# Pooled attention and a SoLU layer on one core: a new order for the first 260 steps

## The chip, the cores and the metric

One NeuronCore of a Trainium2 chip runs the whole program. The metric is its time on the device in microseconds, the median of three runs. The engines are TensorE (PE in the rows), VectorE (DVE), ScalarE (ACT), GpSimd (POOL) and SyncE (SP); each runs its own instructions in order, and they meet at semaphores. All transfers of this kernel are issued from SP's queue, DMA transpositions among them.

## What is computed

```python
# q, k, v: 8 batches x 8 heads x 576 x 64, f32;  w_in 512x1024, w_out 1024x512
k_p = k.reshape(B, H, 72, 8, D).mean(axis=3)
v_p = v.reshape(B, H, 72, 8, D).mean(axis=3)
scores = scale * np.matmul(q, k_p.transpose(0, 1, 3, 2))
attn = np.exp(scores - np.max(scores, axis=-1, keepdims=True))
attn = attn / (np.sum(attn, axis=-1, keepdims=True) + 1e-09)
x = np.matmul(attn, v_p)            # to 4608 tokens x 512
h = x @ w_in
e = np.exp(h - np.max(h, axis=-1, keepdims=True))
solu = h * (e / (np.sum(e, axis=-1, keepdims=True) + 1e-09))
ln = (solu - mean) / np.sqrt(var + 1e-06) * g_ln
out = ln @ w_out
```

## The kernel before

The 4608 tokens are 36 tiles of 128. A group of nine tiles belongs to two batches: four tiles of the first, one that is half of each, four of the second. Every product is made with float16 pairs, a high and a low part, in three passes (high by high, high by low, low by high). The weights come from memory as 8-byte floats, in four quarters of 1 MB each, and are made into such pairs on the chip: ScalarE takes the exponent word (`w_exp`, line 522) and later a sum of magnitudes (`w_abs`), VectorE shifts and joins the words (`w_shift`, `w_tail`), the four bounds give one scale (`w_rmax`, `w_par` on TensorE, `w_all`, `wi_scale` or `wo_scale`), then ScalarE makes the high part (`w_hi`) and the low part comes over TensorE and ScalarE for w_in (`w_res`, `w_lo`) and from VectorE for w_out. `g_ln`, the layer's gain, is loaded by `load_g` (line 609) and enters w_out's scale.

A tile goes through these steps: `q_hi` (ScalarE) and `q_lo` (VectorE for the first four tiles, else POOL) make q's pair, `q_T` transposes it by DMA (line 751); `scores` on TensorE; `s_max`, `s_sub`, `s_exp`, `e_sum`, `e_rec`, `e_mul` make the softmax on VectorE and ScalarE; `e_hi` (ScalarE) and `e_lo` (POOL) its pair, `e_T` transposes it (line 843); `av` multiplies with v (line 853); `x_hi` (ScalarE) and `x_lo` (VectorE) make x's pair; `mm1` multiplies with w_in (line 885, three parts of eight matmuls); `h_max`, `h_exp`, `z_mul`, `z_hi`, `z_cen`, `z_lo`, `z_var` make the layer's z, `z_T` transposes it (line 960); `mm2` multiplies with w_out (line 1017); `o_evac` and `o_store` write the result. Per batch, POOL adds up the groups of eight of k and v (`pool_kv`, line 341, three levels for each of three pieces), VectorE and TensorE find a scale (`a_max`, `a_par`, `a_all`, `a_scale`), and `v_put` on POOL lays v out for `av` in `vb`. For tile 0, `mm1`'s third part needs all low parts of w_in and its second the low part of x.

Buffers set waits as well. The tag `h` in PSUM has two buffers, given in the order of use: four `w_res` of w_in, then `mm1` of tile after tile. The tags `x` (`av`, and the small products for scales) and `s` (`scores`) have one each. q's pairs have two, so `q_hi` waits for the transposition that read the buffer before.

The order of all work is written out by hand. Lines 1044 to 1400 list 2272 steps, each with its engine and what it depends on; `ORDER` (line 25) names them by number, and the loop at the end issues them in that order, so it is the order of each engine's instructions:

```python
    with tc.manual_schedule():
        for n in order:
            ops[n][3](*ops[n][4])
```

So TensorE, VectorE, ScalarE, POOL and SP each see the subsequence of `ORDER` that is theirs. In the kernel before, SP begins with three pieces of k, g, two halves of q (part 0, part 1), a small piece of v, four quarters of w_in, the first quarter of w_out, one half of v, q_T(0), the other half of v, the fourth quarter of w_out, q_T(1), the second quarter, q's mixed tile, the third quarter, a small piece of the next k, q_T(2), a small piece of the next v, e_T(0).

Of the kernel before, what the change touches and what calls it, by code (L numbers as in the profile page):

```python
# [25 lines left out]
    2, 0, 1, 12, 3, 4, 11, 50, 5, 6, 56, 57, 7, 53, 8, 58, 54, 13, 182, 51, 52, 9, 183, 55, 75, 65,  # L26
    59, 184, 113, 185, 76, 186, 60, 66, 187, 188, 61, 190, 77, 62, 63, 17, 64, 189, 191, 236, 192,
    18, 67, 237, 21, 10, 20, 16, 19, 238, 22, 68, 25, 24, 23, 26, 28, 29, 27, 30, 32, 31, 14, 94,
    33, 34, 69, 35, 36, 114, 282, 193, 283, 37, 47, 194, 72, 195, 48, 196, 95, 73, 44, 197, 131,
    74, 198, 41, 199, 70, 200, 15, 97, 71, 331, 134, 38, 284, 239, 115, 78, 201, 79, 39, 137, 240,  # L30
    203, 49, 204, 80, 241, 202, 205, 81, 242, 332, 206, 98, 82, 42, 243, 83, 244, 85, 381, 88, 245,
    89, 129, 99, 86, 90, 40, 382, 130, 246, 91, 333, 383, 102, 285, 384, 385, 93, 45, 386, 286,
    248, 87, 43, 103, 92, 96, 287, 101, 144, 207, 288, 247, 289, 208, 250, 46, 290, 210, 291, 209,
    249, 292, 251, 84, 106, 145, 252, 481, 163, 211, 293, 132, 294, 482, 146, 387, 133, 389, 334,
    107, 483, 104, 212, 390, 335, 484, 108, 336, 297, 296, 253, 213, 337, 164, 295, 254, 298, 338,
    138, 100, 256, 214, 339, 216, 340, 217, 135, 255, 215, 139, 136, 110, 218, 341, 111, 257, 141,
    391, 219, 342, 112, 220, 343, 344, 345, 299, 485, 223, 116, 346, 258, 300, 224, 105, 347, 302,
    117, 259, 227, 225, 303, 123, 226, 301, 486, 260, 109, 142, 229, 120, 304, 262, 221, 263, 487,
    126, 124, 140, 264, 348, 118, 143, 261, 265, 231, 119, 165, 147, 228, 157, 266, 232, 349, 128,
    158, 269, 350, 489, 122, 271, 148, 351, 125, 270, 127, 330, 121, 352, 274, 273, 305, 488, 272,  # L40
    149, 233, 306, 222, 308, 307, 150, 309, 151, 152, 230, 275, 310, 311, 267, 153, 353, 312, 160,
    154, 234, 268, 155, 315, 235, 277, 354, 316, 161, 156, 490, 313, 355, 278, 159, 357, 358, 356,
    388, 162, 359, 317, 319, 166, 537, 362, 279, 360, 276, 361, 491, 318, 314, 167, 392, 280, 492,
    321, 364, 393, 323, 168, 394, 538, 365, 493, 169, 170, 171, 324, 363, 395, 368, 366, 320, 396,
    539, 397, 325, 173, 398, 322, 399, 174, 176, 400, 367, 494, 326, 403, 370, 495, 401, 372, 402,
    496, 404, 178, 405, 175, 497, 373, 179, 636, 498, 377, 586, 499, 180, 327, 500, 177, 501, 374,
    281, 181, 504, 502, 587, 172, 406, 505, 588, 540, 407, 503, 541, 409, 369, 506, 443, 507, 542,
    444, 408, 543, 410, 436, 544, 328, 545, 546, 411, 547, 727, 548, 412, 551, 550, 508, 549, 413,
    552, 589, 509, 371, 553, 414, 590, 415, 511, 637, 416, 591, 380, 375, 417, 418, 592, 512, 419,
    510, 329, 437, 420, 638, 445, 554, 438, 593, 423, 376, 513, 378, 439, 594, 421, 595, 555, 728,  # L50
    425, 424, 596, 557, 427, 556, 597, 514, 599, 598, 428, 426, 729, 558, 515, 730, 516, 440, 429,
    731, 732, 517, 733, 639, 518, 422, 734, 600, 559, 640, 735, 601, 641, 441, 602, 431, 642, 456,
    560, 737, 379, 830, 519, 442, 561, 522, 563, 432, 738, 520, 562, 521, 430, 739, 564, 524, 603,
    565, 566, 523, 567, 831, 433, 604, 526, 525, 457, 643, 832, 644, 568, 606, 570, 645, 528, 646,
    605, 572, 571, 527, 446, 607, 434, 573, 649, 435, 784, 447, 608, 574, 647, 448, 449, 648, 569,
    450, 451, 651, 736, 452, 576, 650, 453, 578, 609, 575, 454, 652, 610, 529, 612, 579, 613, 614,
    459, 455, 615, 611, 577, 580, 530, 879, 617, 616, 462, 653, 581, 583, 460, 633, 532, 654, 463,
    655, 461, 464, 740, 458, 619, 785, 533, 741, 620, 465, 531, 786, 742, 466, 534, 467, 623, 743,
    632, 468, 469, 470, 744, 472, 622, 624, 621, 656, 745, 746, 747, 473, 584, 475, 474, 748, 787,
    749, 476, 751, 535, 657, 788, 750, 752, 789, 702, 753, 618, 658, 790, 929, 479, 791, 625, 792,  # L60
    478, 627, 793, 794, 682, 477, 659, 795, 585, 480, 833, 582, 798, 660, 628, 662, 661, 663, 664,
    834, 880, 796, 835, 754, 686, 881, 665, 836, 666, 629, 797, 626, 755, 635, 756, 669, 683, 837,
    757, 671, 670, 838, 667, 684, 630, 930, 758, 799, 931, 689, 800, 674, 932, 933, 934, 703, 839,
    840, 687, 759, 634, 1029, 842, 471, 631, 690, 841, 688, 783, 672, 882, 760, 677, 673, 883, 845,
    675, 668, 884, 844, 801, 761, 885, 763, 678, 705, 764, 802, 886, 935, 887, 691, 762, 765, 685,
# [108 lines left out]
def kernel(  # L174
# [102 lines left out]
    bat = {b: {} for b in range(B)}  # L277
# [1165 lines left out]
```

## Time and profile before

| | |
|---|---|
| time, median of 3 runs | 480.87 us (480.17 to 481.0) |
| the profiled execution, its time | 481.14 us |
| its span, first to last instruction | 479.4 us |
| TensorE busy | 443.1 us, 92% of the span |
| VectorE, ScalarE, POOL busy | 341.4, 354.1, 349.7 us |
| granted TensorE clock | 1.000 over the span |
| DMA share, share of the 16 engines' span | 80.2% |

The span is the part between the first and the last instruction of the profiled execution; 1.74 us lie around it. A busy share is a mean over the whole span, while the work differs: in the first 45 us TensorE is far from full, and from 120 us on it has hardly a gap. In the rows, a timeline's line gives the start, the time, the engine, the line of the kernel, the tiles written and read, and in brackets how long the engine stood before it and what ended that wait. `xN` is a group of N instructions in one line. Starts are from the span's start.

### The profile page before, as it was taken

The numbers are of one execution on the slowest core, as the hardware profiler recorded it, in microseconds if no ns is written. First come the engines' busy times: TensorE is split into PE (matmuls) and PEld (weight loads), VectorE is DVE, ScalarE is ACT, GpSimd is POOL, SyncE is SP. The second block draws the span as 40 slices with busy tenths as digits, with TensorE's granted clock in tenths as the row PEclk, the third lists the DMA queues.
The fourth block names the chain that finished last, engine by engine and source line by source line (L and its number), as shares of the span: only waits on it lengthen the run. The fifth ranks groups of instructions, "written<-read, shape, count | busy, mean of one in ns | idle before, by whom it ended". The sixth has DMA issues, their size and how long they took to land.

```text
span 479.4 us, 9043 instructions
## 1 busy us (share of the span) xinstructions
PE 443.1 (92%) x3100; PEld 230.1 (48%) x3100; DVE 341.4 (71%) x835; ACT 354.1 (74%) x593; POOL 349.7 (73%) x489
## 2 busy tenths in 40 slices
PE   0167999999999999999999999999999999999996
PEld 0033544555455555554545544555545554545462
DVE  2989998599668876677668975787657886783620
ACT  1789999769976687767876698677776688666751
POOL 6256789968999897997989568996999538535340
PEclk9999999999999999999999999999999999999999
DMA  8999864899989999889978888889997648435451
GB/s 253 418 348 214 227 120 109 174 236 230 194 210 204 218 167 235 173 209 198 208 164 198 187 196 177 200 178 220 195 203 166 151 101 145 111 85 130 92 137 58
DMA packets 201390, 89.14 MB, mean 186 GB/s; under 512 B 177664, under 2 KB 186112, under 8 KB 200832
## 3 DMA queue, kind: packets, MB, share of 16 engines
q1 hardware_dynamic: 201344, 88.57, 80.2%
q8 instruction: 24, 0.39, 0.4%
q14 instruction: 22, 0.18, 0.1%
HBM read 36.70 MB, written 9.44 MB: 96 GB/s over the span
## 4 chain that ended last, share of the span: by engine, by line
PE 78%; DMA 8%; DVE 5%; ACT 5%; issue 2%; SPq 1%; POOL 0%; ACTq 0%; POOLq 0%
PE op L1017 35%; PE hp L885 34%; PE xp L853 6%; DMA qT<-q 4%; PE sc L763 3%; DMA eT<-e 2%; DMA qr<-in_q_dram 2%; DVE wo L689 1%; DVE m L895 1%; DMA zT<-z 1%; DVE u_wo L536 0%; ACT osb L1025 0%; ACT junk L965 0%; ACT xT L861 0%; ACT q L734 0%
## 5 line engine op out<-in xcount | busy, mean ns | idle before, releaser
L1017 PE MATMUL op<-wo,zT 128*128 128x512 f16 (+1 forms) x888 | 197.3, 373 | 1.4 <-DMA zT<-z 0.8
L885 PE MATMUL hp<-wi,xT 128*128 128x512 f16 x864 | 195.8, 379 | 2.7 <-ACT xT L861 2.7
L885 PEld LDWEIGHTS <-xT 128*128 128x128 f16 x864 | 82.7, 98 | 97.8 <-ACT xT L861 3.3
L1017 PEld LDWEIGHTS <-zT 128*128 128x128 f16 x888 | 84.4, 98 | 92.0 <-DMA zT<-z 1.9
L952 POOL TENSOR_TENSOR z<-z,z 128x512 f16<-128x512 f32 x71 | 82.2, 1169 | 42.5 <-ACT z L939 42.2
L895 DVE TENSOR_REDUCE m<-hp 128x1 f32<-128x1024 f32 x36 | 44.0, 1223 | 28.2 <-PE hp L885 28.1
L341 POOL TENSOR_TENSOR vr<-vr 128x512 f32<-128x512 f32 (+3 forms) x48 | 48.1, 1006 | 14.6 <-DMA vr<-in_v_dram 14.0
L832 POOL TENSOR_TENSOR e<-e,e 128x512 f16<-128x512 f32 x36 | 41.6, 1155 | 22.6 <-ACT e L825 22.4
L944 ACT ACTIVATE z<-z,sz 128x1024 f16<-128x1024 f32 x36 | 41.2, 1145 | 17.6 <-DVE z L930 17.4
L906 ACT ACTIVATE z<-hp,nb,Hb 128x1024 f32<-128x1024 f32 x32 | 38.4, 1199 | 15.0 <-DVE nb L898 14.2
L930 DVE SCALAR_TENSOR_TENSOR z<-hp,rs,z 128x1024 f32<-128x1024 f32 x36 | 46.1, 1280 | 3.4 <-ACT z L906 2.0
L341 POOL TENSOR_TENSOR kr<-kr 128x512 f32<-128x512 f32 (+3 forms) x48 | 42.3, 890 | 4.3 <-DMA kr<-in_k_dram 3.7
L774 DVE TENSOR_REDUCE mx<-sc 128x8 f32<-128x576 f32 x36 | 27.2, 754 | 23.8 <-PE sc L763 23.4
L939 ACT ACTIVATE z<-z,sz 128x1024 f32<-128x1024 f32 x36 | 41.1, 1143 | 0.7
L1025 ACT ACTIVATE osb<-op,f 128x512 f32<-128x512 f32 (+1 forms) x37 | 24.7, 667 | 20.0 <-PE op L1017 11.8
L853 PEld LDWEIGHTS <-vb 128*128 128x128 f16 x640 | 35.2, 98 | 8.8 <-DMA eT<-e 1.2
L853 PE MATMUL xp<-eT,vb 128*128 128x128 f16 (+1 forms) x640 | 38.2, 214 | 0.2
L965 ACT ACTIVATE junk<-z 128x1024 f16<-128x1024 f32 x36 | 37.7, 1047 | 0.2
L744 POOL TENSOR_TENSOR q<-qr,q 128x512 f16<-128x512 f32 x28 | 32.3, 1156 | 6.8 <-ACT q L734 6.8
L788 DVE TENSOR_REDUCE sc<-sc 128x8 f32<-128x576 f32 x36 | 27.4, 762 | 13.5 <-ACT sc L784 13.3
L861 ACT ACTIVATE xT<-xp 128x512 f16<-128x512 f32 x36 | 21.3, 592 | 15.3 <-PE xp L853 14.9
L763 PEld LDWEIGHTS <-qT 128*128 128x128 f16 (+1 forms) x640 | 23.1, 103 | 12.1 <-issue 3.8
(232 smaller groups left out, 588.2 us busy)
## 6 DMA issues: line engine op xcount, KB each, us to landing
kr<-in_k_dram SPq DMA_DIRECT2D x16, 512.0 KB, 4.4
qr<-in_q_dram SPq DMA_DIRECT2D x16, 512.0 KB, 4.9
vr<-in_v_dram SPq DMA_DIRECT2D x16, 512.0 KB, 4.9
out_dram<-osb SPq DMA_DIRECT2D x31, 256.0 KB, 3.0
wor<-in_moe_w_out_dram SPq DMA_DIRECT2D x4, 1024.0 KB, 9.2
wo<-in_moe_w_in_dram SPq DMA_DIRECT2D x2, 1024.0 KB, 8.2
wir<-in_moe_w_in_dram SPq DMA_DIRECT2D x2, 1024.0 KB, 12.1
out_dram<-osb SPq DMA_DIRECT2D x10, 128.0 KB, 2.3
```

The lines of the kernel that those rows point to most:

```text
L341: nc.gpsimd.tensor_tensor(out=dst, in0=src[:, :, :n], in1=src[:, :, n : 2 * n], op=ALU.add)
L832: nc.gpsimd.tensor_tensor(out=m[:, 1], in0=e_pair(i)[:, :, :P], in1=m[:, 0], op=ALU.subtract)
L853: nc.tensor.matmul(xp[:, c, lo:hi], lhsT=vb[b % 2][:, x, c].rearrange("p j d -> p (j d)"), rhs=eT[:, e, lo:hi], start=(n == 0), stop=(n == 3),
L885: nc.tensor.matmul(hp[:, f], lhsT=xT[:, xt, c], rhs=wi[:, wt, c, f * 512 : (f + 1) * 512], start=(part == 0 and n == 0), stop=(part == 2 a ...
L895: nc.vector.tensor_reduce(out=small(i, "m"), in_=tl[i]["hp"], axis=AX.XY, op=ALU.max)
L906: nc.scalar.activation(z, t["hp"], AF.Exp, bias=t["nb"], scale=hsc(i, 0), accum_out=small(i, "se"))
L930: nc.vector.scalar_tensor_tensor(out=t["z"], in0=t["hp"], scalar=t["rs"], in1=t["z"], op0=ALU.mult, op1=ALU.mult, accum_out=small(i, "sz"),)
L939: nc.scalar.activation(t["zf"], t["zf"], AF.Identity, bias=t["sz"], scale=-float(DFF))
L944: nc.scalar.activation(t["z16"][:, 0], t["zf"], AF.Identity, bias=t["sz"], scale=-float(DFF))
L952: eng.tensor_tensor(out=t["z16"][:, 1, fs], in0=t["zf"][:, fs], in1=t["z16"][:, 0, fs], op=ALU.subtract)
L965: nc.scalar.activation(junk, t["zf"], AF.Square, scale=DFF**-0.5, accum_out=small(i, "V"))
L1017: nc.tensor.matmul(op_, lhsT=zT[:, zt, c], rhs=wo[:, wt, c, cols(hf)], start=(part == 0 and n == 0), stop=(part == 2 and n == len(todo) - 1),)
```

## The change

The first 260 entries of `ORDER` are a new permutation of the same 260 steps; entry 261 and all behind it are as before. No step, duration or buffer is added or taken away. Two conditions in the code let a part that is not part 0 come first. By engine, what moves:

- SP: three pieces of k, q's part 1, q's part 0, the small piece of v, four quarters of w_in, q_T(0), both halves of v, q_T(1), the fourth and the first quarter of w_out, q's mixed tile, the second quarter, q_T(2), e_T(0), the third quarter, a small piece of the next k, g, q_T(3), e_T(1), and then the other loads of the next batch between e_T(2), q_T(4), z_T(0) and e_T(3).
- VectorE: q's two maxima and its scale before k's; `w_tail` of w_in's fourth quarter behind `s_sub`(1); tile 0's softmax around w_in's scale; `a_max` and `a_scale` of v ahead of tile 1's `s_max`; `w_tail` of w_out's third and fourth quarter ahead of `h_max`(0), where they stood behind `wo_scale`; the maxima of the next batch's q behind `z_mul`(0); g's maximum behind `h_max`(0) and its reduction (`g_all`) just ahead of `z_mul`(0).
- ScalarE: `s_exp`(0) ahead of w_in's high parts, `kv_ps` and `v_hi` of v sooner, `x_hi`(0) ahead of the low parts of w_in's fourth and third quarter, `w_exp` of w_out's third and fourth quarter between these two; `s_exp`(3) behind `x_hi`(1); `z_hi`(0), `z_cen`(0), `x_hi`(2) in this order, where it was `z_hi`(0), `x_hi`(2), `z_cen`(0).
- TensorE: w_in's `w_res` in the order of quarters 1, 2, 4, 3 (it was 4, 1, 2, 3), with `scores`(2) ahead of the last two and `av`(0) between them; `mm1`(0) is cut by `scores`(3) after its first part; g's product and w_out's `w_par` stand between the parts of `mm1`(1); then `mm1`(1)'s third part, `av`(2), `mm1`(2) (it was `av`(2), `mm1`(1)'s third part, `mm1`(2)).
- POOL: the additions in a slightly different order, `e_lo` and the additions for the next batch exchanged in places.

```diff
 ORDER = (
-    2, 0, 1, 12, 3, 4, 11, 50, 5, 6, 56, 57, 7, 53, 8, 58, 54, 13, 182, 51, 52, 9, 183, 55, 75, 65,
-    59, 184, 113, 185, 76, 186, 60, 66, 187, 188, 61, 190, 77, 62, 63, 17, 64, 189, 191, 236, 192,
-    18, 67, 237, 21, 10, 20, 16, 19, 238, 22, 68, 25, 24, 23, 26, 28, 29, 27, 30, 32, 31, 14, 94,
-    33, 34, 69, 35, 36, 114, 282, 193, 283, 37, 47, 194, 72, 195, 48, 196, 95, 73, 44, 197, 131,
...
+    2, 0, 50, 51, 56, 52, 1, 4, 183, 53, 57, 54, 3, 182, 58, 11, 184, 5, 55, 75, 65, 66, 76,
+    185, 186, 187, 188, 59, 60, 190, 191, 61, 62, 6, 7, 63, 64, 236, 8, 17, 192, 18, 20, 237,
+    189, 67, 19, 68, 193, 9, 77, 10, 21, 22, 25, 26, 24, 23, 28, 29, 27, 69, 30, 331, 31, 238,
+    194, 70, 72, 195, 196, 33, 71, 34, 35, 73, 74, 36, 282, 41, 197, 16, 198, 199, 200, 37, 239,
+    38, 201, 202, 78, 203, 44, 13, 131, 79, 283, 14, 80, 81, 240, 82, 83, 85, 94, 241, 242, 39,
+    42, 32, 284, 332, 205, 204, 243, 244, 245, 206, 381, 86, 84, 87, 89, 47, 88, 246, 15, 40,
+    95, 98, 382, 43, 383, 285, 286, 384, 48, 287, 247, 288, 97, 91, 90, 93, 92, 207, 96, 208,
+    134, 385, 289, 248, 386, 290, 12, 249, 49, 291, 99, 209, 250, 292, 101, 102, 45, 333, 210,
...
     def load_q(eng, b, part):
-        if part == 0:
+        if "q" not in bat[b]:
             bat[b]["q"] = p2.tile([P, H, 4, D], F32, tag="qr", name=f"qr{b}")
...
     def z_T(i, x):
         t = tl[i]
-        if x == 0:
+        if "zT" not in t:
             t["zT"] = p3.tile([P, 2, CO, P], F16, tag="zT", name=f"zT{i}")
```

In these numbers 5 to 8 are w_in's quarters, 13 to 16 w_out's, 9 to 11 v's pieces, 12 is g; 192, 238, 284 and 333 are q_T of tiles 0 to 3, 206 and 252 e_T of tiles 0 and 1.

## Rows read from the trace of the kernel before

**Rows 1.** Stretches: us, busy PE, PEld, DVE, ACT, POOL (instructions); clock, DMA share, GB/s.

```profile
6.00:8.00 2.00, 0.00 (x0) 0.00 (x0) 0.00 (x0) 0.00 (x0) 1.92 (x4) 1.00 0.91 197
16.00:18.00 2.00, 0.00 (x0) 0.00 (x0) 1.86 (x3) 2.00 (x4) 0.00 (x0) 1.00 0.99 418
30.00:40.00 10.00, 6.71 (x34) 2.75 (x32) 9.84 (x23) 9.93 (x16) 4.81 (x8) 1.00 1.16 312
120.00:240.00 120.00, 120.00 (x850) 62.33 (x849) 87.68 (x219) 91.82 (x155) 108.58 (x149) 1.00 0.95 201
```

**Rows 2.** Chain that ended last, in order of time: start us, us, what.

```profile
15.91 10.68 DMA qT<-q
...
31.05 9.48 DMA qT<-q
```

**Rows 3.** TensorE's timeline, 40 to 66 us: start, us, what [idle before, releaser].

```profile
40.57 0.69 PE L763 MATMUL sc<-kT,qT 128*128 128x72 f16 x16 [1.40 <-DMA qT<-q]
...
43.42 1.05 PE L853 MATMUL xp<-eT,vb 128*128 128x128 f16 x16
...
45.97 3.63 PE L885 MATMUL hp<-wi,xT 128*128 128x512 f16 x16 [1.50 <-ACT xT L861]
...
53.67 1.90 PE L885 MATMUL hp<-wi,xT 128*128 128x512 f16 x8 [0.82 <-ACT xT L861]
...
58.09 7.07 PE L885 MATMUL hp<-wi,xT 128*128 128x512 f16 x32
...
65.89 3.62 PE L1017 MATMUL op<-wo,zT 128*128 128x512 f16 x16
```

**Rows 4.** VectorE's timeline, 9 to 59 us, same columns.

```profile
9.90 1.22 DVE L360 TENSOR_REDUCE amx_q<-qr 128x1 bf16<-128x1024 f32 x1 [7.76 <-DMA qr<-in_q_dram]
11.73 1.22 DVE L360 TENSOR_REDUCE amx_q<-qr 128x1 bf16<-128x1024 f32 x1 [0.61 <-DMA qr<-in_q_dram]
...
18.56 0.69 DVE L536 TENSOR_SCALAR u_wi<-u_wi 128x1024 int32<-128x1024 int32 x1
...
29.50 1.11 DVE L536 TENSOR_SCALAR u_wo<-u_wo 128x1024 int32<-128x1024 int32 x1
...
41.31 0.76 DVE L774 TENSOR_REDUCE mx<-sc 128x8 f32<-128x576 f32 x1 [0.91 <-PE sc L763]
...
50.98 0.41 DVE L382 TENSOR_REDUCE pq('b', 1)_548<-gq('b', 1)_532 128x1 f32<-128x256 f32 x1
...
56.07 1.28 DVE L930 SCALAR_TENSOR_TENSOR z<-hp,rs,z 128x1024 f32<-128x1024 f32 x1
...
58.61 1.22 DVE L557 SCALAR_TENSOR_TENSOR wor<-wor,u_wo 128x1024 int32<-128x1024 int32 x1
```

**Rows 5.** ScalarE's timeline, 14 to 60 us.

```profile
14.37 0.72 ACT L734 ACTIVATE q<-qr,sq('b', 0)_178 128x512 f16<-128x512 f32 x1 [2.46 <-DVE sq('b', 0)_178 L394]
...
21.81 1.21 ACT L524 ACTIVATE u_wi<-wir 128x1024 f32<-128x1024 f32 x1 [0.25 <-DMA wir<-in_moe_w_in_dram]
...
44.17 0.72 ACT L784 ACTIVATE sc<-sc,ct('b', 0)_203 128x576 f32<-128x576 f32 x1 [0.79 <-DVE sc L777]
...
53.03 0.58 ACT L861 ACTIVATE xT<-xp 128x512 f16<-128x512 f32 x1
...
57.40 1.15 ACT L944 ACTIVATE z<-z,sz 128x1024 f16<-128x1024 f32 x1 [0.61 <-DVE z L930]
...
59.97 5.33 ACT L660 ACTIVATE wo<-wor,sg_wo 128x512 f16<-128x512 f32 x8
```

**Rows 6.** POOL's timeline, 25 to 30 us.

```profile
25.66 1.27 POOL L341 TENSOR_TENSOR vr<-vr 128x512 f32<-128x512 f32 x1 [10.80 <-DMA vr<-in_v_dram]
27.86 2.19 POOL L341 TENSOR_TENSOR vr<-vr 128x512 f32<-128x512 f32 x2 [0.94 <-DMA vr<-in_v_dram]
```

**Rows 7.** SP's issues, 29 us: start us, issue us, what.

```profile
28.99 1.35 SPq L513 DMA_DIRECT2D wor<-in_moe_w_out_dram  x1
```

**Rows 8.** L513 at that issue: microseconds until it landed.

```profile
DMA to landing us min/median/max: 10.0/10.0/10.0
```

259 rows, old and new, of the table ORDER are left out of this document.

## The prediction

> **What bounds the kernel now.** I read the stretches of the span first [rows 1]: TensorE is full for 120.00 of the 120 us from 120 to 240, so every microsecond by which its dense work starts earlier comes off the end, and little else does. The question is when the dense work begins, and the change rewrites just that part. The ramp has two limits. Up to about 40 us it is the one SyncE (SP) queue: the order of its issues sets the order of the landings, and the stretches show the DMA busy at about 1.0. In the chain that ended last, q's first transposition takes 10.68 us from issue to landing and its third 9.48, the longest pieces of the ramp [rows 2]. From 30 us on ScalarE (9.93 of 10 us) and VectorE (9.84) are full as well [rows 1], so work comes earlier only if their waits shrink. TensorE's own timeline gives the milestones [rows 3]: scores of tile 2 at 40.57, after 1.40 of waiting for q's transposition; `av` of tile 0 at 43.42; the first product with w_in, mm1(0), at 45.97; mm1(1) at 53.67 after an idle 0.82; mm1(1)'s last third and all of mm1(2) from 58.09; the first product with w_out at 65.89.
>
> **The front of the queue.** g (4 KB, the only load of single 4-byte elements) leaves its place ahead of q. No row prices it alone. From 6 to 8 us the queue moved 197 GB/s where it moves 418 later: a loss of 2 x (1 - 197/418) = 1.06 us, and at most the whole stretch, 2.0 [rows 1]. I take 1.3, near the lower end, because data did move in it. q's halves, at 9.90 and 11.73 before [rows 4], land at 8.6 and 10.4, and ScalarE's q_hi(0), at 14.37 before [rows 5], comes at 13.07. The last quarter of w_in, at 21.81 before [rows 5], lands at 20.5. Where g goes, behind w_out's third quarter and one piece of k, it delays q_T(3) by the same 1.3; that lands near 43 and is wanted near 44.5.
>
> **q_T(0) ahead of w_out and v.** It landed at 15.91 + 10.68 = 26.6, behind w_in, one quarter of w_out and half of v; v's half was there at 25.66 [rows 6], so the transposition itself added 1.0. Now only w_in is ahead: 20.5 + 1.0 = 21.5. VectorE is busy with shifts of w_in until about 22.5, so tile 0's softmax starts without the wait and falls into gaps, where it stood behind w_in's scale. SP stands longer at this issue (it needs q_lo(0), about 14.4) with v's two halves queued behind it; w_in fills the queue until 20.5, so no data is late for that.
>
> **v sooner.** POOL had v's second half at 27.86 after a wait [rows 6]; right behind q_T(0) both halves are there by 24.2. v's scale comes near 31 and the last v_put near 37.5. That is worth nothing by itself: av(0) has another releaser, q_T(2), below.
>
> **One quarter of w_out behind e_T(0).** The queue up to q_T(2) is as before less g (1.3), one quarter of w_out (1 MB at 418 GB/s, 2.5) and one small piece of k (0.3): 40.55 - 4.1 = 36.45. Bounds: not before tile 1's scores leave their buffer, about 35.6; at worst its old 9.48 from an issue near 29.4, 38.9. I take 36.45, since the items ahead of it are the same ones. Then TensorE runs in order: scores(2) and one w_res in 43.42 - 40.57 = 2.85, av(0) in 1.05, the other w_res in 2.85 - 0.69 = 2.15 [rows 3]. mm1(0) starts at 36.45 + 6.05 = **42.5** against 45.97, 3.5 earlier. x_hi(0), and the w_lo that frees mm1's buffer, fall beside the second w_res.
>
> **ScalarE to x_hi(1).** Before, it ran from 14.37 to 53.03 [rows 5] with four waits, 2.35 in all (0.25 the first, 0.79 the last): 36.3 us of work. s_exp(3), 0.72, goes behind. After: 13.07 + 36.3 - 0.7 + 0.95 of waits left (w_in's scale 0.6, w_abs 0.2, v's scale 0.15, from laying out its new order) = 49.6. x_hi(1) ends at 50.1 and mm1(1) starts at **50.15** against 53.67, still 3.5.
>
> **VectorE to z_mul(0).** From 9.90 to 56.07 [rows 4] it is 46.2 us, with six waits (0.61 the first, 0.91 the last) of 2.8. Two w_tails come ahead and two maxima of q go behind, all 1.22, which cancels; q's reduction over both (0.41) and w_out's (half the columns, 0.3 by my estimate) go behind: -0.7. New waits: q's second half 0.6, the round trip over TensorE for q's scale 0.4, q_hi 0.35, w_in's scale 0.4, scores(2) 0.65, together 2.4. So 8.6 + 46.2 - 2.8 - 0.7 + 2.4 = **53.7**, only 2.4 earlier.
>
> **The new wait.** Before, mm1(1)'s last third stood between av(2) and mm1(2). Now mm1(2) follows av(2) at once, and its x_hi(2) stands on ScalarE behind z_hi(0) and z_cen(0). z_mul to z_hi was 57.40 - 56.07 = 1.33; z_hi, x_hi and z_cen together were 59.97 - 57.40 = 2.57 [rows 4, 5]: 53.7 + 3.9 = 57.6, with the hand-over to TensorE 57.75. Before it was 58.09 + 1.73 (a quarter of that row's four passes) = 59.82. TensorE idles over 1 us there, and the lead falls to **2.1**. w_hi for w_out, at 59.97 before, follows at 57.9, the same lead, and mm2(0), which needs it, comes 2.1 earlier. Past that point the orders are the same on every engine, all lead by 2 or more, and TensorE is full.
>
> **Sum.** -3.5 at mm1(0), +1.4 given back at mm1(2): -2.1. The profiled execution took 481.14 (span 479.4 and 1.74 around it), 0.27 above the median of 480.87; it would be 479.0, and the median **478.8**.
>
> **VectorE against POOL.** A w_shift took 0.69 at 18.56 and 1.11 at 29.50, while POOL ran v's additions until 30.05 [rows 4, 6]: 0.42 for one collision. The four shifts of w_out meet other POOL work after the change, so this costs between -0.4 (that one gone) and 1.7 (four of them). I take 0. The Trainium skill (SBUF — State Buffer, section "SBUF: two separate sides") says VectorE and GpSimd share one port pair, which an instruction holds alone until it ends while the other engine stands; the 1.11 agrees with that. The rule speaks against laying v's additions beside VectorE's chain: by it the sum would shrink from -2.1 towards -0.4, by the row of one collision it stays.
>
> **The rivals.**
> - The lead of 3.5 survives: the waits of VectorE and ScalarE are shorter than I laid out, and mm1(2) does not idle. For it: each wait is an estimate. Against: x_hi(2) is behind two passes on ScalarE by the order itself. 477.4.
> - The lead is eaten, or the new order does not make the transpositions land sooner: q_T(2) at its late bound (2.4 later) or four collisions (1.7). For it: SP stood 9 to 11 us on transpositions, more than the data ahead of them explains by itself. 480.6.
> - Slower, by w_out's third quarter. Its load can no longer be issued before e_T(0), which waits for POOL's e_lo(0). On ScalarE w_exp for it stands ahead of w_exp for the last quarter, w_lo(2), which mm1(0)'s last third needs, and x_hi(1). Its turn comes at about 42. The load took 10.0 us from its issue at 28.99 [rows 7, 8]; from an issue near 34.6 that is 44.6, 2.6 late, and leaves a gain of under 1. Every microsecond past 42 delays x_hi(1) by as much. It decides from a landing at 45.5 on; if e_T(0) is held up 2 to 3 us it costs 4 to 5.5 in place of the 2.1: 482.5. Against: the queue ahead is short by then, and by the rate it lands at about 40.3.
>
> **Numbers.** Forecast 0.52 (own range 477.7 to 479.9), lead survives 0.13, eaten 0.22, slower 0.13. Leaving out the far ends of the first and the last, 476.9 to 481.6 holds 8 in 10. About 0.2% (1 us) is what a measurement of this kernel can tell from no change. Faster by more than that: 0.64; within: 0.22; slower: 0.14.
>
> **What would show it.** Right: q_T(0) landing near 21.5, scores(2) near 36.5, mm1(0) near 42.5, mm1(1) near 50, an idle of about 1 us before mm1(2) released by ScalarE, the first product with w_out near 63.8, nothing different in kind after 120. Wrong: a wait of ScalarE for w_out's load near 42; q_hi(2) or q_hi(3) held, ahead of w_in's scale, by a transposition still in flight; w_par for w_out held on TensorE by g's late reduction, which now holds the same PSUM buffer just before it; or a gap between 65 and 120 that gives the lead back.

## The result: slower, 483.7 us

The changed kernel takes 483.7 us in the median (480.65 to 487.09), the kernel before 480.87: so it loses 2.8; the ratio of the means (484.07 to 480.89) is 1.0066, 95% interval 1.0041 to 1.0091. The forecast was 478.8 and faster, the range ended at 481.6. The profiled execution of after took 485.99 us, with a span of 484.3, which is 4.9 longer than that of before: the lines below account for this one execution, and others lost less.

TensorE's timeline of after holds the milestones of the prediction (start us, us, what [idle before, releaser]):

```profile
22.17 1.14 PE L770 MATMUL sc<-kT,qT 128*128 128x72 f16 x16 [7.90 <-DMA qT<-q]
36.44 0.68 PE L770 MATMUL sc<-kT,qT 128*128 128x72 f16 x16 [0.52 <-DVE e L810]
...
42.81 1.89 PE L892 MATMUL hp<-wi,xT 128*128 128x512 f16 x8
...
50.59 1.90 PE L892 MATMUL hp<-wi,xT 128*128 128x512 f16 x8 [0.69 <-ACT xT L868]
...
57.80 1.90 PE L892 MATMUL hp<-wi,xT 128*128 128x512 f16 x8 [0.85 <-ACT xT L868]
65.17 0.37 PE L376 MATMUL gq('b', 1)_686<-identb,amx_q 128*128 128x128 bf16 x2 [5.47 <-DVE xT L872]
65.34 5.84 PE L892 MATMUL hp<-wi,xT 128*128 128x512 f16 x16
71.01 1.06 PE L860 MATMUL xp<-eT,vb 128*128 128x128 f16 x16
71.91 3.62 PE L1024 MATMUL op<-wo,zT 128*128 128x512 f16 x16
```

Down to the row at 57.80 this is the forecast, and ahead of before [rows 3]: scores(2) 36.44 for 40.57, mm1(0) 42.81 for 45.97, mm1(1) 50.59 for 53.67. Then TensorE stands 5.47 us, a pass of 16 matmuls takes 5.84 instead of 3.62, and the first product with w_out starts at 71.91, where before had it at 65.89. What it waited for is on VectorE, and its cause on POOL. First VectorE:

```profile
53.60 1.28 DVE L937 SCALAR_TENSOR_TENSOR z<-hp,rs,z 128x1024 f32<-128x1024 f32 x1
...
57.27 6.13 DVE L647 TENSOR_SCALAR sg_wo<-g_sb,sw_wo 128x8 f32<-128x8 f32 x1
63.31 1.21 DVE L367 TENSOR_REDUCE amx_q<-qr 128x1 bf16<-128x1024 f32 x1
64.44 0.67 DVE L872 SCALAR_TENSOR_TENSOR xT<-xp,xT 128x512 f16<-128x512 f32 x1
```

and POOL beside it:

```profile
56.59 1.14 POOL L839 TENSOR_TENSOR e<-e,e 128x512 f16<-128x512 f32 x1
57.70 1.14 POOL L959 TENSOR_TENSOR z<-z,z 128x512 f16<-128x512 f32 x1
58.82 0.31 POOL L348 TENSOR_TENSOR kp<-kr 64x64 f32<-64x64 f32 x1
59.09 1.14 POOL L959 TENSOR_TENSOR z<-z,z 128x512 f16<-128x512 f32 x1
60.21 0.71 POOL L348 TENSOR_TENSOR kr<-kr 128x256 f32<-128x256 f32 x1
60.89 0.85 POOL L348 TENSOR_TENSOR kp<-kr 128x128 f32<-128x128 f32 x2
61.71 0.44 POOL L348 TENSOR_TENSOR vp<-vr 32x128 f32<-32x128 f32 x1
62.12 2.06 POOL L348 TENSOR_TENSOR vr<-vr 128x512 f32<-128x512 f32 x2
```

`sg_wo`, a product of 128x8 numbers inside `wo_scale`, takes 6.13 us; before it took 0.22, at 58.48. Nothing it reads is late (runs 1 and 2). It stands while POOL runs nine instructions one right behind the other, and is done between the two additions of v at 62.12, where the row breaks: the second reads what the first wrote, and starts 0.08 after its end. Before, POOL had a wait of 2.03 at that place, for z_cen(0) on ScalarE (VectorE's and POOL's rows of before):

```profile
58.48 0.22 DVE L640 TENSOR_SCALAR sg_wo<-g_sb,sw_wo 128x8 f32<-128x8 f32 x1
```

```profile
60.14 2.28 POOL L952 TENSOR_TENSOR z<-z,z 128x512 f16<-128x512 f32 x2 [2.03 <-ACT z L939]
```

Two parts of the change close this gap. z_mul(0), which stood only 2.4 us ahead of `sg_wo`, comes 2.47 forward (53.60 for 56.07 [rows 4]) and `sg_wo` only 1.2. And ScalarE now makes z_cen(0) ahead of x_hi(2), not behind it, so that z_cen(0) starts at 56.11 where before had it at 58.93:

```profile
56.11 1.15 ACT L946 ACTIVATE z<-z,sz 128x1024 f32<-128x1024 f32 x1
57.16 0.58 ACT L868 ACTIVATE xT<-xp 128x512 f16<-128x512 f32 x1
```

So z_lo(0) and k's additions now run when `sg_wo` asks. By my estimate from these rows, with x_hi(2) still first z_lo(0) could have started only near 58.7, and POOL would have stood from 57.74 (56.59 + 1.14) until then, with `sg_wo` asking since 57.27. No run undid this exchange. Behind `sg_wo` stand, on VectorE, x_lo(2), which mm1(2) needs, and, on ScalarE, w_hi of w_out:

```profile
63.43 5.25 ACT L667 ACTIVATE wo<-wor,sg_wo 128x512 f16<-128x512 f32 x8 [5.55 <-DVE sg_wo L647]
```

The stretches (us; busy PE, PEld, DVE, ACT, POOL with instructions; granted clock, DMA share, GB/s) show what the pause cost on top: the clock falls to 0.50, the lower level, 1.2 GHz, and is back at 70.

```profile
62.00:64.00 2.00, 0.00 (x0) 0.00 (x0) 2.00 (x2) 0.57 (x1) 1.92 (x3) 0.75 1.05 292
64.00:66.00 2.00, 0.83 (x4) 0.46 (x4) 2.00 (x3) 2.00 (x4) 0.17 (x1) 0.50 0.35 74
66.00:68.00 2.00, 2.00 (x6) 0.69 (x5) 1.97 (x12) 2.00 (x5) 0.00 (x0) 0.50 0.03 8
68.00:70.00 2.00, 2.00 (x7) 0.70 (x6) 1.99 (x6) 2.00 (x5) 0.00 (x0) 0.54 0.00 0
70.00:72.00 2.00, 2.00 (x23) 1.41 (x22) 1.86 (x3) 0.91 (x2) 0.00 (x0) 1.00 0.00 0
```

The sum at the first product with w_out: forecast 63.8, plus 5.9 (6.13 less 0.22), plus 2.2 (5.84 less 3.62) is 71.9. That it closes to a tenth is in part luck: with `sg_wo` out of the way this product came at 63.42 (run 1), and from there 0.4 stays unexplained. From 120 us on TensorE is as full as before (120.00 of the 120 us to 240), so most of the lateness stays: 6.0 at this product, 5.4 at the one that before had at 115.39, 4.9 in the span.

### The profile page after: what moved, and what is told of

The parts are those of the page before. It is cut to its first block, busy times and chain, and to the rows that moved or that the text cites. A ratio compares the mean times of both kernels' runs of the same rounds, so it can differ in the third digit from the quotient of the medians.

```text
span 484.3 us, 9040 instructions
## 1 busy us (share of the span) xinstructions
PE 445.5 (92%) x3100; PEld 231.6 (48%) x3100; DVE 346.4 (72%) x835; ACT 353.9 (73%) x593; POOL 346.5 (72%) x489
## 4 chain that ended last, share of the span: by engine, by line
PE 83%; DVE 6%; ACT 4%; DMA 3%; POOL 2%; issue 1%; SPq 0%; ACTq 0%; DVEq 0%
PE op L1024 36%; PE hp L892 36%; PE xp L860 6%; PE sc L770 3%; DMA qr<-in_q_dram 2%; DVE sg_wo L647 1%; DMA eT<-e 1%; DVE amx_q L367 1%; ACT ab_wi L554 1%; POOL e L839 0%; DVE e L810 0%; ACT u_wi L531 0%; DVE sc L795 0%; ACT sc L791 0%; DVE xT L872 0%
## 5 line engine op out<-in xcount | busy, mean ns | idle before, releaser
L892 PE MATMUL hp<-wi,xT 128*128 128x512 f16 x864 | 198.3, 382 | 2.0 <-ACT xT L868 1.9
L959 POOL TENSOR_TENSOR z<-z,z 128x512 f16<-128x512 f32 x71 | 81.9, 1165 | 52.2 <-ACT z L946 51.9
L348 POOL TENSOR_TENSOR kr<-kr 128x512 f32<-128x512 f32 (+3 forms) x48 | 40.8, 860 | 3.5 <-DMA kr<-in_k_dram 3.0
L770 PE MATMUL sc<-kT,qT 128*128 128x72 f16 (+1 forms) x640 | 25.6, 201 | 11.9 <-DMA qT<-q 7.9
```

Of the source, the lines that this page charges most:

```text
L348: nc.gpsimd.tensor_tensor(out=dst, in0=src[:, :, :n], in1=src[:, :, n : 2 * n], op=ALU.add)
L770: nc.tensor.matmul(sc[lo:hi, h // HB, (h % HB) * SP : (h % HB + 1) * SP], lhsT=t["qT"][:, h, lo:hi], rhs=bat[b]["kT"][:, x, hc], start=(x ...
L892: nc.tensor.matmul(hp[:, f], lhsT=xT[:, xt, c], rhs=wi[:, wt, c, f * 512 : (f + 1) * 512], start=(part == 0 and n == 0), stop=(part == 2 a ...
L959: eng.tensor_tensor(out=t["z16"][:, 1, fs], in0=t["zf"][:, fs], in1=t["z16"][:, 0, fs], op=ALU.subtract)
```

## The experiments

The numbers of the runs are theirs in this section; a letter for a theory means what the expectation beside it says. Two theories stood at first. **Port**: `sg_wo` stands because POOL holds what both need, and without that the forecast holds. **Late input**: `sg_wo` waits for something else. In the diffs, numbers are entries of `ORDER`: 345, 346 e_lo(3, 0), (3, 1); 226, 227 z_lo(0, 0), (0, 1); 139 to 143 and 146 `pool_kv` of k's next batch (142 is (kr, 1, 1); 143, (kr, 1, 2), reads what 142 writes); 165, 157, 158 `pool_kv` of v.

**1. `sg_wo` on ScalarE, ahead of w_hi.**

```diff
-        nc.vector.tensor_scalar(out=sg, in0=g_sb, scalar1=sw, scalar2=None, op0=ALU.mult)
+        nc.scalar.activation(sg, g_sb, AF.Copy, scale=wst["wo"]["sw"])   # in the first w_hi
```

> The changed kernel with one instruction moved: w_out's scale times g (128x8, written by VectorE in wo_scale, 6.13 us in the changed kernel, 0.22 in the one before) is made by ScalarE just ahead of its first reader. Theory 1 (POOL's unbroken row of instructions from 48.1 to 64.2 us keeps that VectorE instruction out): the stall is gone, VectorE's next instructions come at about 57.3, no other VectorE instruction takes over 2 us there, mm1(2) does not stop for 5.5 us, and the lead of about 2 us forecast before shows: 478.3 to 479.2 us, with little spread. Rival 2 (VectorE stands at that time or place for another reason, such as g's data or a fetch of instructions): another VectorE instruction near 57 us takes the 5 to 6 us, and the time stays at 482 to 486. Rival 3 (the loss is not the stall but the new order as such): the stall goes and the time stays above 481.

480.22 us, ratio 0.9989 [0.9979, 0.9998]. TensorE's pause is gone, the clock stays at 1.00 and the first product with w_out starts at 63.42, a lead of 2.5 over before. But VectorE now stands one step later, at the first w_lo of w_out (VectorE's timeline):

```profile
60.64 3.03 DVE L698 SCALAR_TENSOR_TENSOR wo<-wor,sg_wo,wo 128x512 f16<-128x512 f32 x1
...
63.67 1.15 DVE L698 SCALAR_TENSOR_TENSOR wo<-wor,sg_wo,wo 128x512 f16<-128x512 f32 x1
...
64.86 0.74 DVE L698 SCALAR_TENSOR_TENSOR wo<-wor,sg_wo,wo 128x512 f16<-128x512 f32 x1
```

0.74 is its time alone. z_mul(1) is late behind it, and TensorE waits 1.47 us before the small product at 68.51. At the product that before started at 115.39, 1.2 of the 2.5 are left (114.17).

**2. `sg_wo` on VectorE, in eight products of 128x1.**

```diff
+        for n in range(CO):
+            nc.vector.tensor_scalar(out=sg[:, n : n + 1], in0=g_sb[:, n : n + 1], scalar1=sw, ...)
```

> The changed kernel with the same 128x8 product written by VectorE as eight instructions of 128x1. In the profile of the changed kernel 128x1 instructions of VectorE ran in 0.15 to 0.21 us beside POOL's row. Theory 1, with the port depending on the form: no stall, eight times 0.2 us, some 1.4 us later on VectorE than without it, 479 to 480.5 us. Rival 2 (any instruction that stands there waits): the first of the eight takes 5 to 6 us, 482 to 487.

480.21 us, 0.9989 [0.9978, 1.0]. The eight take 1.05 us together, while POOL runs as before: the same engine, inputs and place, so a late input is out. Only the wider form stands. The first w_lo then takes 1.78.

**3. The kernel before, with k's additions ahead of z_lo(0).**

```diff
-345, 346, 227, 226, 142, 140, 143, 165, 157, 158
+345, 346, 142, 140, 143, 165, 227, 226, 157, 158
```

> The kernel before with one thing added: POOL's four small additions for the next batch stand ahead of z_lo(0), so that POOL is not idle from 58.1 to 60.1 us, where VectorE's 128x8 product took 0.22 us at 58.5. Everything else is as before. Theory 1: that product is held, by 0.5 us (until the end of the one POOL instruction it meets) up to 4 us (until the row ends), ScalarE's w_hi follows it late, and the time grows by 0.5 to 4 us: 481.3 to 485. Rival 2 and 3: 0.2 us as before, 480.5 to 481.2.

482.28 us, 1.0042 [1.0026, 1.0057]. `sg_wo` was let in (0.34 us); a w_tail of w_out behind it was not, and took 3.70 us where it takes 1.57 in before:

```profile
61.80 3.70 DVE L552 SCALAR_TENSOR_TENSOR wor<-wor,u_wo 128x1024 int32<-128x1024 int32 x1
```

So the wait can be had in the kernel before by moving four of POOL's additions, and costs about what it lasts (2.1 us longer, 2.0 by the ratio). Which instruction is hit differs.

**4. A bench: nine POOL additions (128x512) in a train, behind the last store of before.** The whole time says nothing here; each VectorE instruction starts when the first addition is done.

```diff
+        for kind in (8, 8, 1, 8, "shift", 8, "max", 8, "tail", 8, 512, "shift", 8, "tail"):
+            gpsimd.tensor_tensor(first = a + b)
+            for _ in range(8): gpsimd.tensor_tensor(rest = a + b)     # one place, nine times
+            vector: first[:, :kind] * s, or a shift, a maximum, a w_tail, of first
```

> The kernel before with a measurement behind its last store: fourteen times POOL runs nine additions of 128x512 f32 without a wait between them (1.2 us each, 10.5 in all), and VectorE starts one instruction when the first of them is done. In turn: products 128x8 f32 by a scalar from memory (six times between the others), 128x1, 128x512, shifts of 128x1024, a maximum over 128x1024, a shift-and-or of two 128x1024. Its time is that of the measurement and says nothing. Theory 1: the products of 128x8 and 128x512 and the shifts last far longer than alone, until the row ends (up to 9.5 us) or until some end of a POOL instruction in it; 128x1 and the maximum last as alone (0.2 and 1.2 us). If the port goes to whoever asks at the end of one instruction: at most 1.2 us longer, every time. If it is a matter of chance: different lengths for the six equal ones. Rival 2: all as alone.

A 128x8 product took 1.21 us every time, one addition long; a 128x1 product 0.21 and a maximum 1.22, as alone. That is a wait for one instruction, not for a train, and did not explain 6.13. POOL's rows showed the difference: the eight additions write one place, so each is recorded 0.08 after the end of the one before it, while those of the kernels are recorded 0.03 *before* that end. Theory A: VectorE is let in only where POOL waits for its own result.

**5 and 6. Such a pair put early, or late, into POOL's train of after.**

```diff
-346, 345, 227, 146, 226, 142, 140, 143, 165
+346, 345, 142, 143, 227, 146, 226, 140, 165      # early
+346, 345, 227, 146, 226, 142, 143, 140, 165      # late
```

> The kernel after, with two of GpSimd's additions brought forward: pool_kv(1, kr, 1, 1) and pool_kv(1, kr, 1, 2), which reads what the first writes, stand directly behind e_lo(3, 0). Nothing else moves, and no operation is added or left out. Theory A (VectorE is let in only where GpSimd's next instruction waits for the result of the one before it; in the trace of after such a pair is recorded 0.08 us apart, all others overlap by 0.03): sg_wo starts at 57.3 and gets in behind the first addition, at 58.4, so it takes 1.2 to 1.4 us instead of 6.13; w_hi(wo) from 58.6, the first mm2 at 64.4, 480.2 to 481.2 us. Theory B (VectorE is out until the train is through, or until the v additions at its end, whatever the order): sg_wo still takes some 6 us, 483 to 484 us. Theory C (let in at random at the end of any instruction): no change of the chance, some other duration.

> The kernel after, with two neighbours of GpSimd's train exchanged: pool_kv(1, kr, 1, 2) directly behind pool_kv(1, kr, 1, 1), whose result it reads, and pool_kv(1, kr, 0, 2) behind both. Theory A: GpSimd now waits for its own result at about 60.9, where it did not in after, and sg_wo gets in there: 3.7 to 3.9 us instead of 6.13, w_hi(wo) from 61.2, an idle TensorE of about 3 us, 481 to 482.5 us. Theory B: 6.1 us and 483 to 484 us. Together with the kernel in which the pair stands early the dose decides: by A 1.3, 3.8 and 6.1 us.

Early: 480.56 us, 1.0004 [0.9992, 1.0016], `sg_wo` 0.77 us. Late: 482.81, 1.0054 [1.0039, 1.0069], `sg_wo` 3.88, as forecast. POOL and VectorE of the late one:

```profile
60.09 0.71 POOL L336 TENSOR_TENSOR kr<-kr 128x256 f32<-128x256 f32 x1
60.88 0.87 POOL L336 TENSOR_TENSOR kp<-kr 128x128 f32<-128x128 f32 x2
```

```profile
56.96 3.88 DVE L635 TENSOR_SCALAR sg_wo<-g_sb,sw_wo 128x8 f32<-128x8 f32 x1
```

60.09 + 0.71 is 60.80, and the next starts at 60.88: the break. `sg_wo` ends at 60.84. But the early one was let in at the end of e_lo(3, 0), one instruction ahead of the pair, where nothing broke. "Only" is too much. Nor do 0.77, 3.88 and 6.13 us show that the place of the break sets the length: in run 16 the unchanged order of after was let in at the end of this same addition, without a break behind it, after 3.90 us. What speaks for the break as a limit is the times: all four executions of the late pair are at most 483.35 us, and 12 of the 16 of after are above that.

**7. A second bench: trains that nothing breaks.**

```diff
+  free:  eight additions 128x256 into eight places;  chain: all into one place
+  pair:  as free, the sixth adds to what the fifth wrote
```

> The kernel before, with 14 trains of nine GpSimd additions (128x256 f32, some 0.72 us each) behind the last store, and one VectorE instruction for each train that starts when the first addition is done. free: the eight others write eight places and none reads what another wrote. chain: all eight add to one place. pair: as free, but the sixth adds to what the fifth wrote. Theory A: a 128x8 product takes some 5.7 us in a free train (the eight additions), under 0.9 in a chain, some 3.5 to 3.7 in a train with a pair; a 128x1024 shift 1.2 more than to the same point; a 128x1 product 0.2 everywhere. Theory B (out for the length of the train): 5.7 in free and pair, and the chain of the earlier bench (1.21 us each time) stays unexplained. Theory C (any end of an instruction): 0.7 in all.

0.67 us for the product in all three kinds, one addition long; the shifts 1.19 to 1.20. Theory A falls: no pair is needed to be let in.

**8. `sg_wo` on ScalarE, the late pair, and two w_lo moved behind x_lo(3).**

```diff
 # VectorE
-w_lo(2, 0), w_lo(0, 0), w_lo(0, 1), a_max(k), z_mul(1), w_lo(3, 1), x_lo(3), ...
+w_lo(2, 0), a_max(k), z_mul(1), w_lo(3, 1), x_lo(3), w_lo(0, 0), w_lo(0, 1), ...
```

> The kernel after, with sg_wo made by ScalarE in front of w_hi(wo), the same exchange of two GpSimd additions, and two of VectorE's w_lo(wo) (0, 0 and 0, 1) moved behind x_lo(3), so that z_mul(1) no longer stands behind them. Theory A, and that the lead of 2.5 us at the first mm2 was eaten by w_lo in the kernel with sg_wo on ScalarE: the first w_lo takes under 1.2 us instead of 3.03, z_mul(1) starts at 64.2 to 64.5 instead of 65.92, the idle TensorE of 1.47 us before a_par(k, 1) is under 0.3, 478.3 to 479.6 us. Rival: the lead is lost behind it anyway (TensorE waits for z_T or w_lo at the next product), 480.0 to 480.5 us as with sg_wo on ScalarE alone.

481.65 us, 1.0024 [1.0012, 1.0036]. The first w_lo took 0.94, z_mul(1) started at 64.27, and the 1.47 before the small product were gone, as expected; yet it is slower. Six w_lo now stand in one block on VectorE, two of them beside z_lo(1) (1.65 us each for 0.74), and h_max(2) and mm2(0)'s last part behind them. TensorE's row of it:

```profile
72.67 1.46 PE L1014 MATMUL op<-wo,zT 128*128 128x512 f16 x6 [1.49 <-DVE wo L686]
```

ScalarE waited 3.06 us at 74.16 for the same reason. The move had made the neighbour late.

**9. A third bench: kinds of POOL instruction, and later requests.**

```diff
+  free as above;  half: f16 subtractions 128x512;  kv: additions in place;  mix: half and kv by turns
+  in front of each product 0 to 4 maxima of 1.22 us
```

> The kernel before, with 14 trains of nine GpSimd instructions behind the last store and a 128x8 VectorE product for each, in front of which stand 0 to 4 VectorE maxima (1.2 us each alone), so that the product asks for the port at different places of the train. free: additions 128x256 f32 into eight places; half: subtractions 128x512 of f16 from f32 with an f16 result, as z_lo; kv: additions in place with two rows of blocks, as pool_kv; mix: both by turns, as in the train of the kernel after. Theory D (what counts is how close GpSimd's instructions stand, not what they are: in the kernels' traces VectorE missed the end of an instruction only where the next is recorded 0.031 to 0.034 us before that end, and was let in where it is 0.035 to 0.046 before or 0.08 behind): the product takes more than one GpSimd instruction only in trains that show that spacing. Theory E (kind: the f16 subtractions or the in-place additions don't let go): long waits in half or kv or mix, none in free, wherever the product asks. Theory F (place: only a request early in a GpSimd instruction is heard, as all those of the earlier bench were): long waits with 1 to 4 maxima in all kinds, none with 0. If no train shows a wait of more than one instruction, the cause lies in what else runs in the kernel (other engines, transfers), and stays open.

Nine of the 14 products were let in at the end of the POOL instruction that ran when they asked. Five stood until the train's last instruction was done: 1.80 in free, 3.98 in half, 4.36 in kv (with no maximum ahead), 2.97 and 4.23 in mix. All four kinds show it, so theory E falls; the spacing is the same in both cases, so D falls; kv's miss asked 0.07 us into an addition, so F falls too.

**10. `sg_wo` on ScalarE and the late pair, VectorE's order as in after.**

> The kernel after with sg_wo made by ScalarE and the two GpSimd additions exchanged (kr 1, 2 directly behind kr 1, 1), VectorE's order as in after. The first w_lo(wo) at 60.8 takes under 1 us, as in the kernel with its w_lo moved (0.94), z_mul(1) starts at 64.3 to 65 instead of 65.92, and the idle TensorE before a_par(k, 1) falls from 1.47 to under 0.5 us; h_max(2) stays at 69 to 71, ahead of where the moved w_lo pushed it (72.54). Theory A: 0.8 to 1.2 us under the kernel with sg_wo on ScalarE alone, 479.0 to 479.6 us. Rival (the gain is lost again before 120 us, in z_T or the stores): 480.0 to 480.4 us.

479.51 us, 0.9975 [0.996, 0.9989]: faster than both kernels. TensorE's rows:

```profile
64.06 3.62 PE L1014 MATMUL op<-wo,zT 128*128 128x512 f16 x16
67.95 0.22 PE L364 MATMUL gk<-identb,amx_k 128*128 128x128 bf16 x1 [0.28 <-DVE xT L862]
```

The first w_lo took 0.81 and the wait of 1.47 fell to 0.28. One w_lo still stood 1.3 us, at 63.00.

**11. `sg_wo` on ScalarE, g's load back at the front.**

```diff
 # SP
-load_kv(0, kr, 1), load_q(0, 1), ...
+load_kv(0, kr, 1), load_g, load_q(0, 1), ...
```

> The kernel after with sg_wo made by ScalarE, and load_g put back to the front of SP's queue, behind load_kv(0, kr, 1), as in before: one part of the change undone. By the prediction's first term q_T(0), scores(0) and all that follows come 1.06 to 2.0 us later (1.3 taken), so mm1(0) at 43.8 instead of 42.52 and 481.0 to 482 us. Rival (other waits take the place, g's load was hidden): mm1(0) within 0.3 us of 42.5 and no difference from the kernel with sg_wo on ScalarE alone.

481.37 us, 1.0008 [0.9994, 1.0022]. mm1(0) at 43.27, scores(0) at 22.41. In the eleven profiled executions that have g late, after and its variants, mm1(0) starts between 42.44 and 43.45 and scores(0) between 21.78 and 22.72, so this one doesn't stand out. The medians of this run and of run 1, 481.37 and 480.22, say little of a term of this size: they are of two sessions (by the ratios to before the difference is 0.9), and the profiled execution here was the fastest of its ten. The landings tell more: the last quarter of w_in was there at 20.92 in the mean (20.66 to 21.62) in those eleven, and at 21.60 (21.36 to 21.78) in the seven that have g at the front. So g's load there costs some 0.7; the lower bound of the prediction was 1.06.

**12. A fourth bench: the moment of the request**, 34 trains, the second maximum wider by 56 or 76 columns from one to the next.

> The kernel before, with 34 trains of nine GpSimd instructions behind the last store (13 trains of f16 subtractions 128x512, 13 of free additions 128x256, 8 of additions in place), and in each a 128x8 VectorE product behind two maxima; the second maximum is 56 or 76 columns wider from train to train, so that the product asks at another moment of the GpSimd instruction that runs. Theory G (one chance): the product is let in either at the end of the instruction that runs when it asks, or only when the train breaks or ends; no train shows it let in between. Under it the moment decides: asked over 0.7 us ahead of that end it was let in 10 of 10 times in the earlier benches, nearer than 0.65 us in some and in some not, so misses are expected among the late requests alone. Theory H (chance at each end): waits of two or three instructions in many trains, and no dependence on the moment. Theory E (kind): all misses in the f16 subtractions and the additions in place, none in the free additions.

VectorE's rows at neighbouring moments (0.44, 0.51, 0.59 and 0.68 us into a POOL instruction of 1.15):

```profile
480.59 7.41 DVE L1447 TENSOR_SCALAR b_out<-b_first,b_out 128x8 f32<-128x8 f32 x1
...
490.45 0.67 DVE L1447 TENSOR_SCALAR b_out<-b_first,b_out 128x8 f32<-128x8 f32 x1
...
500.08 0.59 DVE L1447 TENSOR_SCALAR b_out<-b_first,b_out 128x8 f32<-128x8 f32 x1
...
509.73 7.17 DVE L1447 TENSOR_SCALAR b_out<-b_first,b_out 128x8 f32<-128x8 f32 x1
```

21 of 34 were let in at the first end, one at the second, and 12 only when the train ended, 2.57 to 7.41 us. H falls. The misses asked 0.09 to 0.96 us ahead of the first end, the 21 let in there 0.16 to 1.12, so the moment doesn't tell them apart, and neither does the kind (5, 4 and 3 misses in half, free and kv). They come in nearly every third train: with at most 15 POOL instructions in a row since the last break, 45 of the 48 products of 128x8 in the four benches were let in at the first end, with more, 1 of 16 (the expectation of run 13 counts a few other forms too).

**13. A break ahead of the request.**

```diff
-141, 163, 138, 164, 145, 139, 346, 345, 227, 146, 226, 142, 140, 143, 165
+141, 142, 163, 138, 164, 145, 139, 346, 345, 227, 146, 226, 140, 143, 165
```

> The kernel after, with one GpSimd addition brought forward: pool_kv(1, kr, 1, 1) directly behind pool_kv(1, kr, 1, 0), whose result it reads, so that GpSimd waits 0.08 us for itself at about 54.6, some 2.7 us before sg_wo asks. Nothing else moves, and nothing follows sg_wo's request that would break GpSimd's row earlier than in after (the v additions at 63). Theory I (length of the row: in the benches the product was let in at the end of the running instruction in 38 of 41 cases with up to 15 GpSimd instructions in a row behind the last break, and had to wait for the next break in 16 of 17 with more): sg_wo asks as the sixth or so and is let in at the end of e_lo(3, 0), in 0.4 to 1.3 us instead of 6.13; the first mm2 at 63.8 to 64.5, 480.2 to 481.2 us. Rival (the length is not what counts, the two numbers fell together; the moment within the instruction or chance decides): 5 to 6 us as in after, 483 to 484 us.

485.25 us, 1.0113 [1.0079, 1.0147]. The break came at 52.2, and `sg_wo` asked as the seventh in the row; it took 5.13 us all the same. Theory I falls for the kernel. POOL and VectorE:

```profile
61.80 0.44 POOL L336 TENSOR_TENSOR vp<-vr 32x128 f32<-32x128 f32 x1
62.21 2.07 POOL L336 TENSOR_TENSOR vr<-vr 128x512 f32<-128x512 f32 x2
```

```profile
57.14 5.13 DVE L635 TENSOR_SCALAR sg_wo<-g_sb,sw_wo 128x8 f32<-128x8 f32 x1
```

It ended at 62.27, between two additions that follow each other without a break (61.80 + 0.44 is 62.24, the next starts at 62.21).

**14 to 16. The kernel after, three executions more.**

> The kernel after, unchanged, profiled in another execution. Theory J (what decides is the moment at which sg_wo asks, finer than the order of the instructions fixes it): the 6.13 us of the first profile is one outcome among several; in this and two further executions sg_wo takes between 0.4 and 6.2 us and not the same each time, and the time of each execution follows it, 480.5 to 481 us where it takes under 1.3, 485 to 487 where it takes over 5. Theory K (the order and the row of GpSimd fix it): 5.9 to 6.2 us in all three, and what spreads the times of after from 480.65 to 487.09 us lies elsewhere.

> As the run before it: the kernel after in a further execution. Theory J: sg_wo anywhere from 0.4 to 6.2 us, the time following it. Theory K: 5.9 to 6.2 us.

> As the two runs before it: the kernel after in a further execution. Theory J: sg_wo anywhere from 0.4 to 6.2 us, the time following it. Theory K: 5.9 to 6.2 us.

```profile
56.94 6.41 DVE L647 TENSOR_SCALAR sg_wo<-g_sb,sw_wo 128x8 f32<-128x8 f32 x1
```

```profile
56.92 6.38 DVE L647 TENSOR_SCALAR sg_wo<-g_sb,sw_wo 128x8 f32<-128x8 f32 x1
```

```profile
57.72 3.90 DVE L647 TENSOR_SCALAR sg_wo<-g_sb,sw_wo 128x8 f32<-128x8 f32 x1
```

486.26, 486.79 and 485.54 us. The first two were let in where after was, at the break between the two additions of v. The third ended at 61.62; POOL's rows beside it:

```profile
60.88 0.71 POOL L348 TENSOR_TENSOR kr<-kr 128x256 f32<-128x256 f32 x1
61.56 0.86 POOL L348 TENSOR_TENSOR kp<-kr 128x128 f32<-128x128 f32 x2
```

60.88 + 0.71 is 61.59, and the next starts at 61.56: an unbroken end. The same program gives 6.4 or 3.9, so the order alone doesn't fix it: theory K falls, and J holds as far as three executions go. None of them was an execution of 481 us, so that those are the ones in which `sg_wo` was let in at once is likely, not shown. One sign for it: of the 13 executions in the result, the three with a granted clock of 1.000 are the three fastest (480.65, 481.9, 482.0), and the ten others have 0.991 to 0.996.

**What is settled and what is open.** The loss is `sg_wo` standing behind POOL: it goes when ScalarE makes `sg_wo` or VectorE makes it in 128x1 pieces (1, 2), and such a wait can be made in before (3). That a break in POOL's row limits it fits every run: in runs 1 and 3, too, the held w_lo and w_tail ended only 0.55 and 1.08 us behind v's first addition (63.12 and 64.42), where the row breaks, which is no more than they last alone (0.74 and 1.22). It was not shown apart from chance (6, 16). What decides, at the end of a POOL instruction in an unbroken row, between letting VectorE in and running on is open. Kind, moment and spacing sort none of the cases. The length of the row sorts the benches (45 of 48 against 1 of 16) and failed in the one execution of the kernel that tried it (13).

## Why the prediction was wrong

- **Queue, q_T(0), q_T(2).** scores(0) 22.17 (the landing of q_T(0) forecast at 21.5, measured 22.1), scores(2) 36.44 (36.45), mm1(0) 42.81 (42.5): right. At scores(2) it was partly luck: q_T(2) landed at 36.14, and what scores(2) waited for last was VectorE's use of tile 1's scores (L810), in the forecast only a lower bound of about 35.6. The term for g's load, 1.3 with a lower bound of 1.06, was too dear: by the landings of w_in it is some 0.7 (run 11).
- **v sooner.** Taken as worth nothing by itself. No run took it alone, so it is neither shown nor refuted.
- **x_hi(1), z_mul(0), the new wait.** mm1(1) 50.59 (50.15), z_mul(0) 53.60 (53.7), mm1(2) 57.80 (57.75) with an idle 0.85 released by ScalarE (forecast: over 1): right. The lead of 2.1 existed at that point: 2.0 (57.80 for 59.82).
- **w_hi(wo), the first product with w_out.** 63.43 (57.9) and 71.91 (63.8): wrong, by `sg_wo`. With it on ScalarE they came at 57.53 and 63.42.
- **VectorE against POOL: the step that failed.** I named the mechanism, put it at 0, and bounded it at 1.7, as four shifts of 0.42 each. Three things were off. The price of one collision came from one row ([rows 4]: the shift at 29.50), where POOL's row broke behind the addition that it met (that ended at 30.06, the next started at 30.13); a row that runs on can cost several times that. I looked at the shifts alone, because they are long, and not at every VectorE form that was ever held; the one hit lasts 0.22 us alone. And the gap of POOL in which `sg_wo` had run was closed, by z_mul(0) coming forward by more than `wo_scale` and by z_cen(0) going ahead of x_hi(2); I priced that exchange for mm1(2) alone, and did not ask what then stands beside `sg_wo`. The term measured 5.9 at `sg_wo`, plus 2.2 by the clock.
- **"Past that point the orders are the same, all lead by 2 or more, and TensorE is full."** Right for the orders, wrong for the lead. With `sg_wo` out of the way, 1.2 of 2.5 were left at 114 us, because the same collision hit w_lo; with the pair as well, 1.7 of 1.8 were left in the profiled execution (113.66 for 115.39), and 1.2 in the median (0.9975).
- **The rivals.** w_out's third quarter landed at 41.6, and ScalarE did not wait for it: that rival was wrong. The slower case I gave a chance had another cause. "Lead eaten", 480.6, is about what remained in runs 1, 2 and 5 (480.22, 480.21, 480.56), but not for the reasons it names: not q_T(2) and not four shifts, but a w_lo that was held (3.03 and 1.78 us for 0.74 in runs 1 and 2).

The Trainium skill (SBUF — State Buffer, section "SBUF: two separate sides") says that of a VectorE and a GpSimd instruction which need the shared port pair the one that starts first keeps it for the whole instruction. By that rule `sg_wo` would have stood 0.5 us, to the end of e_lo(3, 0); the first bench agrees (1.21, one addition of 1.26), and after does not: 6.13 us, over nine instructions. The measurement decides: the wait can last longer than one instruction.

## What to carry over

A short VectorE instruction that stands alone between two engines' chains is priced by the row of GpSimd work beside it, not by its own length: list each such instruction with what GpSimd will be running when it comes, and take the rest of that unbroken row as its upper bound. When a change brings one chain forward by more than another, look for the idle time of a third engine that the second was living in. If a small product on a critical chain can be made by ScalarE, or in 128x1 pieces, that bound goes away for it, and the next instruction behind it has to be asked about in its turn (the w_lo of runs 1 and 2).

## What was not expected of the hardware

- One 128x8 product stood 3.9 to 6.4 us in four executions of one program, over up to nine POOL instructions, and 0.22 in another order; 128x1 products and maxima were never held (0.21 and 1.22 beside POOL, as alone).
- After a pause of TensorE of 5.47 us the granted clock was 0.50 for nearly 7 us (63 to 70) and cost 2.2 us. After a pause of 3.25 us, in the third further execution of after, it was 0.50 too, and a pass took 6.42 us for 3.62; after one of 3.22 in run 6 it stayed at 1.00. So a pause of this length sometimes costs two to three us more than itself; what tells the two apart no row here shows.
